# A first batch kept on the chip: block transposes in place of two trips through DRAM in a spectral mixing and feed-forward kernel

## The chip, the cores and the metric

One core of one Trainium2 chip. The metric is the device time in microseconds (us) of one execution. Both kernels were run several times; a run is called fast when it is within 1.5% of the fastest of the same kernel. The engines are TensorE (PE in the profile, PEld for its weight loads), VectorE (DVE), ScalarE (ACT), GpSimd (POOL) and SyncE (SP). A name with a q behind it, such as SPq, is an engine's queue of DMA issues. PSUM is the memory that takes TensorE's products until another engine copies them out, SBUF the one that the engines otherwise read and write. The granted clock is the share of full speed that the profile shows for TensorE.

## The reference, cut to what matters

```python
def _attn_ref(x, filt_r, filt_i):                 # x: 8 batches x 3008 rows x 256 channels
    X = np.fft.rfft(x, axis=1)
    F = (filt_r + 1j * filt_i)[None, :, :]
    y = np.fft.irfft(X * F, n=x.shape[1], axis=1)
    return y.astype(np.float32)

def _moe_ref(x, w_in, w_out, alpha):              # 24064 tokens, 256 -> 2048 -> 256
    h = x @ w_in
    s = np.sin(alpha * h)
    g = h + s * s / (alpha + 1e-09)
    return (g @ w_out).astype(np.float32)
```

The second function is applied to the first one's result. The Fourier transform of length 3008 is split as 47 x 64, so that it becomes matrix products with small tables.

## The kernel before

Each batch goes through four products of the spectral part, and then its rows go through the feed-forward part:

- `first` (profile name `pa<-x`): the transform over 47, for two of the 64 columns at a time;
- `forward` (`pb<-t`): the transform over 64, with the twiddle factors in the table `d_t`. Its 128 output rows are 64 real and 64 imaginary parts;
- the product with the filter on VectorE, then `inverse` (`pc<-p`) with the table `e_t`;
- `last` (`pd<-t`): the inverse transform over 47, which leaves y with the channels on the partitions;
- the feed-forward part: `hidden` (`ph<-y`), a cosine on ScalarE, an add on VectorE, `project` (`po<-v`), in 48 chunks of 16 hidden blocks. A chunk is eight steps of two blocks. One step takes 2.1 to 2.4 us.

Between `first` and `forward`, and between `inverse` and `last`, the axis on the partitions must change. The kernel before does this for every batch with a trip through DRAM: rows are stored in one order (`d<-t`, `d<-g`) and loaded in another (`t<-d`).

```python
        def load_t2(self, g):
            ...
            for p in range(2):
                a0 = p * NS + 6 * g
                eng = nc.gpsimd if self.b else nc.scalar if p else nc.sync
                marks["t2", g] = eng.dma_start(out=self.t2[g][64 * p:64 * p + 64, :, :],
                                               in_=self.d1[a0:a0 + 6, :, :].rearrange("s n c -> n s c"))

        def forward(self, u):
            ...
            nc.scalar.copy(out=self.xf[u], in_=ps)
            if self.fused:
                self.xs[u] = xspool.tile([128, 2, C], FP16, name=f"xs_{b}_{u}", tag="xs")
                for p in range(2):
                    nc.sync.dma_start(out=self.xs[u][64 * p:64 * p + 64, :, :],
                                      in_=self.xf[u][64 - 64 * p:128 - 64 * p, :, :])

        def product(self, u):
            for k in range(1 if self.fused else 2):
                ... tensor_tensor(out=pt, in0=self.xf[u], in1=f_t[k][:, 2 * u:2 * u + 2, :], op=ALU.mult)

        def cross(self, u):                               # only for a fused batch
            xs, p = self.xs[u], self.p[u][0]
            nc.vector.tensor_tensor(out=xs, in0=xs, in1=f_t[1][:, 2 * u:2 * u + 2, :], op=ALU.mult)
            nc.vector.tensor_tensor(out=p, in0=p, in1=xs, op=ALU.add)

        def inverse(self, w):
            ...
            for i in range(2):
                for k, pt in enumerate(pr):               # one product if fused, two if not
                    nc.tensor.matmul(out=ps[:, i, :], lhsT=e_t[:, k, 2 * w + i, :],
                                     rhs=pt[:, i, :], start=(k == 0), stop=(k == len(pr) - 1))
```

A complex product needs each half of the rows (real, imaginary) times the filter's real part, plus the other half times its imaginary part. There are two ways. An **unfused** batch leaves the exchange of the halves to TensorE: the second inverse table has its halves exchanged, which takes 48 inverse products. A **fused** batch exchanges the halves with two DMAs of 64 KB per block (`xs<-xf`), adds on VectorE, and takes 24 inverse products. `FUSED = 2` says that batches 0 and 1 are unfused and the others fused.

Batch 0 stands alone in front of the feed-forward part. The spectral work of batch b then lies between the steps of the feed-forward part for earlier rows, by a table of step numbers:

```python
        for i in range(16):
            put(5 + 0.5 * i if b == 1 else ..., s.first, i, pe=True)
        for g in range(4):
            put(13.5 if b == 1 else max(z + -56, 46.5), s.load_t2, g)
        for u in range(12):
            inv = 22.5 + u if b == 1 else 59 + 2.1 * u if b == 2 else z + -40.8 + 2.3 * u
            fwd = inv - (1.5 if b == 1 else 6)
            put(fwd, s.forward, u, pe=True)
            put(fwd + (0.5 if b == 1 else 1.5), s.product, u)
            if s.fused:
                put(fwd + 4.5, s.cross, u)
            put(inv, s.inverse, u, pe=True)
```

## Time and profile before

| | kernel before |
|---|---|
| time, median of 3 runs | 814.85 us (814.2 to 816.39) |
| span of the profiled run | 812.3 us |
| TensorE busy | 95% of the span |
| first feed-forward product | 53.46 us |
| step 8, first product of the second chunk | 68.10 us |
| last output product | 804.00 us |

The page's first part (busy us, share of the span, instructions) is the first thing to read:

```profile
PE 771.4 (95%) x5649; PEld 527.5 (65%) x5649; DVE 652.4 (80%) x1191; ACT 612.8 (75%) x1200; POOL 65.4 (8%) x111
```

TensorE has only about 41 us in which it is not busy, and most of them lie before step 8. The prediction below shows the other lines. From its marks the kernel divides into four stretches: the start (to the first feed-forward product), the first chunk (to step 8), the long part (to the last output product, 735.9 us), and the tail (8.3 us).

### The profile page before, as it was taken

The page shows a single profiled execution, that of the slowest core. Times are in us where ns is not written, and L with a number is a line of the kernel's source. Part 1 is how long each engine was busy: PE and PEld are TensorE (multiplying, and loading weights), DVE is VectorE, ACT ScalarE, POOL GpSimd, SP SyncE. Part 2 cuts the span into 40 slices and gives each one's busy share as a digit, 9 for nine tenths or more (in the row PEclk, how much of TensorE's full clock was granted, in tenths as well). Part 3 has the DMA queues.
Part 4 walks back from the last instruction along what each step waited for, and adds up shares of the span by engine and source line. Part 5 has one row for each costly group of instructions (what it writes and reads, how often), then busy time and mean ns, then how long its engine had stood idle before and what let it go on. Part 6 is the DMA issues. An engine that isn't in the chain of part 4 may idle for free.

```text
span 812.3 us, 16130 instructions
## 1 busy us (share of the span) xinstructions
PE 771.4 (95%) x5649; PEld 527.5 (65%) x5649; DVE 652.4 (80%) x1191; ACT 612.8 (75%) x1200; POOL 65.4 (8%) x111
## 2 busy tenths in 40 slices
PE   5657999999999999999999999999999999999995
PEld 2324676676666776667667676667667676666674
DVE  3669797789978998789987998779987999777772
ACT  4547787788878888778887887778887887777662
POOL 3210300110020000200002000200002000000000
PEclk9779999999999999999999999999999999999998
DMA  9985755466576465644657554654558333411111
GB/s 213 227 260 132 186 113 148 127 137 141 117 185 149 97 144 126 184 95 95 140 159 178 111 104 116 193 127 104 115 139 214 73 91 84 116 37 40 40 40 46
DMA packets 86201, 104.44 MB, mean 129 GB/s; under 512 B 10388, under 2 KB 72868, under 8 KB 86120
## 3 DMA queue, kind: packets, MB, share of 16 engines
q1 hardware_dynamic: 73904, 73.45, 34.3%
q0 software_dynamic: 10288, 29.11, 18.0%
q10 hardware_dynamic: 1928, 0.86, 0.4%
q8 instruction: 44, 0.72, 0.4%
q14 instruction: 37, 0.30, 0.1%
HBM read 58.02 MB, written 49.81 MB: 133 GB/s over the span
## 4 chain that ended last, share of the span: by engine, by line
PE 88%; DMA 5%; DVE 2%; ACT 2%; issue 1%; POOL 0%; SPq 0%; ACTq 0%; DVEq 0%; POOLq 0%
PE po L383 39%; PE ph L368 38%; PE pa L159 4%; PE pc L210 3%; PE pb L179 3%; PE pd L230 2%; DMA t<-d 2%; DMA x<-in_x_dram 2%; DVE v L372 1%; ACT cos L371 1%; DMA d<-t 1%; ACT t L136 1%; DVE p L193 1%; DMA d<-g 0%; DVE t L138 0%
## 5 line engine op out<-in xcount | busy, mean ns | idle before, releaser
L372 DVE SCALAR_TENSOR_TENSOR v<-cos,ph 128x512 f16<-128x512 f32 (+1 forms) x768 | 483.5, 672 | 119.3 <-ACT cos L371 116.2
L371 ACT ACTIVATE cos<-ph 128x512 f32<-128x512 f32 (+1 forms) x768 | 411.5, 591 | 99.7 <-PE ph L368 98.9
L368 PE MATMUL ph<-y,w 128*128 128x512 f16 (+1 forms) x1536 | 388.5, 375 | 0.8 <-DVE y L138 0.6
L383 PE MATMUL po<-w,v 128*128 128x256 f16 x3008 | 389.0, 272 | 0.0
L383 PEld LDWEIGHTS <-v 128*128 128x128 f16 x3008 | 289.2, 98 | 77.7 <-issue 1.7
L368 PEld LDWEIGHTS <-w 128*128 128x128 f16 x1536 | 148.1, 98 | 104.3 <-issue 3.6
L182 ACT CAST xf<-pb 128x512 f16<-128x512 f32 x96 | 56.9, 594 | 20.4 <-PE pb L179 17.3
L389 ACT COPY o<-po 128x512 f32<-128x512 f32 x96 | 55.6, 579 | 17.9 <-PE po L383 16.3
L136 ACT CAST t<-pa 96x512 f16<-96x512 f32 x88 | 51.2, 585 | 22.8 <-PE pa L159 22.6
L159 PE MATMUL pa<-x,wf_t 94*96 94x512 f16 x128 | 51.0, 408 | 11.7 <-DMA x<-in_x_dram 8.3
L230 PEld LDWEIGHTS <-t 96*128 96x128 f16 x512 | 36.1, 99 | 34.3 <-DMA t<-d 11.0
L170 POOL DMA_DIRECT2D t<-d x56 | 37.0, 676 | 251.1 <-PE ph L368 183.6
L230 PE MATMUL pd<-wi_t,t 96*128 96x94 f16 x512 | 43.0, 208 | 11.5 <-DMA t<-d 10.1
L193 DVE TENSOR_TENSOR p<-xf,filt 128x512 f16<-128x512 f16 x120 | 47.8, 418 | 6.3 <-ACT xf L182 6.1
L136 ACT CAST y<-pd 128x376 f16<-128x376 f32 x82 | 39.3, 480 | 17.0 <-PE pd L230 16.6
L136 ACT CAST g<-pc 128x512 f16<-128x512 f32 x65 | 38.4, 590 | 11.8 <-PE pc L210 11.6
L210 PE MATMUL pc<-p,e_t 128*128 128x256 f16 x240 | 44.0, 278 | 2.7 <-DVE p L193 1.5
L179 PE MATMUL pb<-t,d_t 128*128 128x256 f16 x192 | 38.2, 282 | 5.9 <-DMA t<-d 4.9
L118 POOL DMA_DIRECT2D x<-in_x_dram x32 | 17.0, 536 | 262.8 <-PE pc L210 145.9
L138 DVE CAST t<-pa 96x512 f16<-96x512 f32 x40 | 27.2, 680 | 12.6 <-PE pa L159 12.6
L210 PEld LDWEIGHTS <-e_t 128*128 128x128 f16 x240 | 23.0, 99 | 16.2 <-issue 2.5
L200 DVE TENSOR_TENSOR p<-p,xs 128x512 f16<-128x512 f16 x72 | 30.6, 425 | 2.5
(31 smaller groups left out, 155.2 us busy)
## 6 DMA issues: line engine op xcount, KB each, us to landing
d<-t SPq DMA_DIRECT2D x32, 384.0 KB
d<-g SPq DMA_DIRECT2D x64, 192.0 KB
t<-d SPq DMA_DIRECT2D x32, 384.0 KB
x<-in_x_dram POOLq DMA_DIRECT2D x32, 376.0 KB, 6.2
t<-d POOLq DMA_DIRECT2D x56, 192.0 KB, 7.0
xs<-xf SPq DMA_DIRECT2D x144, 64.0 KB
out_dram<-o SPq DMA_DIRECT2D x72, 94.0 KB
w_in<-in_moe_w_in_dram POOLq DMA_DIRECT2D x2, 1024.0 KB, 8.9
```

The costliest lines, as they stand in the source:

```text
L136: marks["act"] = nc.scalar.copy(out=dst, in_=src)
L159: marks["pe"] = nc.tensor.matmul(out=ps[0:NK, :], lhsT=wf_t, rhs=self.x[ch][:, 2 * j:2 * j + 2, :], start=True, stop=True)
L179: nc.tensor.matmul(out=ps[:, i, :], lhsT=d_t[:, s, :], rhs=self.t2[s // 6][:, s % 6, :], start=True, stop=True)
L182: nc.scalar.copy(out=self.xf[u], in_=ps)
L193: marks["prod", u] = nc.vector.tensor_tensor(out=pt, in0=self.xf[u], in1=f_t[k][:, 2 * u:2 * u + 2, :], op=ALU.mult)
L210: nc.tensor.matmul(out=ps[:, i, :], lhsT=e_t[:, k, 2 * w + i, :], rhs=pt[:, i, :], start=(k == 0), stop=(k == len(pr) - 1))
L230: nc.tensor.matmul(out=psv[:, i, :], lhsT=self.t4[ch][:, 4 * half + i, cb * 128:cb * 128 + 128], rhs=wi_t, start=True, stop=True)
L368: nc.tensor.matmul(out=ps[:, 0:n], lhsT=w1[:, cb, jb * 128:jb * 128 + 128], rhs=y_cols[:, cb, c0:c0 + n], start=(cb == 0), stop=(cb == 1))
L371: nc.scalar.activation(out=cs[:, 0:n], in_=ps[:, 0:n], func=AFT.Sin, bias=float(np.pi / 2))
L372: marks["snake"] = nc.vector.scalar_tensor_tensor(out=v[k][:, jb, 0:n], in0=cs[:, 0:n], scalar=-1.0, in1=ps[:, 0:n], op0=ALU.add, op1=ALU. ...
L383: nc.tensor.matmul(out=pso[k][:, t % 2, :], lhsT=v[k][:, jb, 128 * t:128 * t + 128], rhs=w2[:, jb, :], start=(jb == 0), stop=(jb == 15))
L389: nc.scalar.copy(out=o[:, 0:nb, :], in_=pso[k][:, 0:nb, :])
```

## The change

The intent: take the two DRAM trips of batch 0 out of the start. VectorE transposes 32 x 32 blocks of 4-byte elements (pairs of channels), so batch 0 never leaves the chip. The start is then filled: six PSUM buffers for stage 1, the inverse tables built between its pieces, weights loaded in order of need and scaled on GpSimd and ScalarE, and 14 products without use ("filler") to keep TensorE's clock up. The memory for this is found by dropping the second inverse table after the start, and therefore batch 1 becomes fused. Two more things move: batch 0's last stage takes two products of 64 columns where one of 128 stood, and the short chunk of 384 columns goes from the end of each pair of batches to its middle. The diff, cut to its core (cuts marked by "..."):

```diff
-FUSED = 2
+FUSED = 1
...
-    e_t = cpool.tile([128, 2, NS, 128], FP16)
+    e_t = cpool.tile([128, NS, 128], FP16)
...
     def last(self, u, on_act=None):
             for i in range(4):
-                nc.tensor.matmul(out=psv[:, i, :],
-                                 lhsT=self.t4[ch][:, 4 * half + i, cb * 128:cb * 128 + 128],
-                                 rhs=wi_t, start=True, stop=True)
+                if self.b == 0:
+                    for k in range(2):
+                        nc.tensor.matmul(out=psv[64 * k:64 * k + 64, i, :], lhsT=t4_0[cb][:, n0 + i, :, k],
+                                         rhs=wi0_t, start=True, stop=True)
+                else:
+                    nc.tensor.matmul(out=psv[:, i, :], rhs=wi_t, start=True, stop=True,
+                                     lhsT=t4_h[ch // 2][0:NK, n0 % 16 + i, cb * 128:cb * 128 + 128])
...
-    after(nc.sync.dma_start(out=d_t, in_=d_dram.ap()), marks["x", 1])
+    nc.sync.dma_start(out=d_t, in_=d_dram.ap())
+    x0 = [load_x(0, ch) for ch in range(4)]
...
+    tables = {7: [(0, 0, True), (0, 1, False)], 11: [(0, 2, True), (1, 0, False)], 15: [(1, 1, True), (1, 2, True)]}
+    for i in range(16):
+        own, tag = (fps, "f") if i % 3 == 2 else (hps, "h")
+        ps = own.tile([128, 512], FP32, name=f"pa_0_{i}", tag=tag)
+        nc.tensor.matmul(out=ps, lhsT=wf0_t, rhs=x0[i // 4][:, 2 * (i % 4):2 * (i % 4) + 2, :],
+                         start=True, stop=True)
+        evac(t1_0[:, 2 * i:2 * i + 2], ps.rearrange("p (n c k) -> p n c k", n=2, k=2), i % 2)
+        for e in tables.get(i, ()):
+            inverse_table(*e)
+
+    def turn(dst, src):
+        nc.vector.transpose(out=dst.bitcast(UINT32).rearrange("p s c k -> p c (s k)"),
+                            in_=src.bitcast(UINT32).rearrange("p s c k -> p c (s k)"))
...
-            put(13.5 if b == 1 else max(z + -56, 46.5), s.load_t2, g)
+            put(14.5 if b == 1 else max(z + -56, 46.5), s.load_t2, g)
...
-            inv = 22.5 + u if b == 1 else 59 + 2.1 * u if b == 2 else z + -40.8 + 2.3 * u
-            fwd = inv - (1.5 if b == 1 else 6)
+            inv = 24 + 1.2 * u if b == 1 else 59 + 2.1 * u if b == 2 else z + -40.8 + 2.3 * u
+            fwd = inv - (5 if b == 1 else 6)
```

## The prediction

> **What bounds the kernel now.** I read the page's strip of slices first, then a table by stage, then the timeline of the first 70 us, and last the waits after 80 us.
>
> ```profile
> PE   5657999999999999999999999999999999999995
> PEclk9779999999999999999999999999999999999998
> DMA  9985755466576465644657554654558333411111
> ```
>
> Each digit is a fortieth of the 812.3 us span, 20.3 us. TensorE is busy all the time except in the first three to four slices, where DMA is the full row and the granted clock dips. So the kernel has two parts: a start limited by something else, and a TensorE-bound rest. The table by stage (start:end, length, then busy us and count of PE, PEld, DVE, ACT, POOL, then granted clock, DMA share, GB/s) says so in numbers:
>
> ```profile
> 0.00:12.50 12.50, 4.72 (x10) 1.82 (x11) 1.60 (x4) 4.78 (x8) 6.45 (x16) 1.00 0.86 168
> 12.50:27.50 15.00, 9.45 (x43) 4.44 (x43) 6.64 (x13) 5.83 (x8) 1.11 (x3) 0.81 0.89 237
> 27.50:42.50 15.00, 12.16 (x70) 7.08 (x69) 13.92 (x34) 10.36 (x19) 4.95 (x9) 0.84 1.09 264
> 42.50:53.50 11.00, 2.02 (x20) 1.42 (x19) 5.70 (x10) 1.62 (x4) 1.24 (x2) 0.65 0.80 219
> 53.50:68.10 14.60, 11.38 (x61) 5.13 (x61) 12.69 (x27) 11.57 (x23) 2.02 (x4) 0.91 0.98 248
> 80.00:804.00 724.00, 720.90 (x5382) 500.80 (x5379) 601.48 (x1084) 569.75 (x1122) 49.62 (x80) 1.00 0.50 120
> ```
>
> From 80 to 804 us TensorE lacks 3.1 us in all. Nothing that leaves its instruction stream alone can win more than that there. The reserve lies before 68 us. The chain that ended last (start us, us, what) shows what ends each pause, and the timeline of TensorE where the next part starts:
>
> ```profile
> 17.52 4.90 DMA d<-t
> 22.58 4.31 DMA t<-d
> 44.08 3.19 DMA d<-g
> 47.49 3.84 DMA t<-d
> 53.43 10.46 DMA x<-in_x_dram
> ```
> ```profile
> 53.46 1.87 PE L368 MATMUL ph<-y,w 128*128 128x512 f16 x4 [0.17 <-ACT y L136]
> ...
> 68.10 1.03 PE L368 MATMUL ph<-y,w 128*128 128x512 f16 x4
> ```
>
> The first four lines are batch 0's two trips through DRAM: 9.5 us between stage 1 and the forward transform, 7.8 us between inverse and last stage. The feed-forward part starts at 53.46 us, and its second chunk (step 8, the first with output products between) at 68.1 us.
>
> **What the Trainium skill says.**
> (1) "VectorE: DVE Perf Modes", section "The three transpose paths": VectorE transposes only inside 32x32 blocks, 311 ns for 128x128 bf16 against 390 ns on TensorE. "Vector Engine (DVE) Microarchitecture Reference", section 3.8, adds one element per cycle and lane. No transpose of this kind is in the trace of before. Estimate for 1024 elements at 0.96 GHz: 1.07 us, plus the fixed part of that 311 ns figure (311 - 133 = 178 ns), about 1.2 us.
> (2) "GPSIMD Engine Reference", section 3.1: an fp32 tensor_tensor of 2048 elements takes 4497 ns, about twice VectorE. Estimate: 2.2 ns each, 1.7 us for 768 elements. The trace has no GpSimd arithmetic, so no run shows it yet; VectorE's own product in this role took 681 ns for 512.
> (3) "TensorE: Matmul & The Clock Gate", Part 1: after an idle window of about 3.4 us the array runs at half clock. The trace agrees: granted clock 0.65 from 42.5 to 53.5 us, and four products took 1.87 us at 53.46 but 1.03 us at 68.10.
>
> **The change part by part.**
>
> *Stage 1.* All products of batch 0 use six PSUM buffers, copies alternate between ScalarE and VectorE, and the results stay in SBUF. In before, loads that wait for a free slot show the four x pieces landed by 6.5, 8.3, 10.1 and 12.2 us. The middle table is now loaded beside them from the start; the engines land 0.21 MB of fp16 per us of such casting loads (209 to 212 GB/s), so read 0.42 MB, and the last piece lands near 12.5. Then four products, two copies each on ScalarE (0.58) and VectorE (0.69): the last copy ends near 15.0. The inverse tables (six groups; four on ScalarE at 1.02 us as before) lie between pieces and end near 18 on TensorE and ScalarE, beside the block transposes.
>
> *First DRAM trip removed, block transposes added.* VectorE: 2 x 1.2, a filter copy of 3072 elements (0.55 us for 1536 before; slope 0.4, so 0.95), 2 x 1.2, another 0.95: 6.7 us, 15.0 to 21.7. Before had 17.5 to 27.0. The filters (3.15 MB of fp32 source behind x) need until about 20; the first half is in time.
>
> *Forward, products, inverse.* Per block of four columns: 2 VectorE products at 0.355 us (spacing in runs: 2.09 us for 6), 1 + 3/4 ScalarE copies at 0.54 us (1.07 for 2), 12 TensorE products of 128 columns at about 0.08 (8 table transposes took 0.62). VectorE from 21.7: 24 x 0.355 + 2 x 0.69 = 9.9; ScalarE 21 x 0.54 = 11.3 from about 19; TensorE 144 x 0.08 = 11.5. All three are near each other, so I add 2 us for hand-overs: the last product ends at 33.6. Before, the same stage ran from 27.0 to 42.8, with 8 filter copies (4.4 us) on a VectorE that was 93% busy.
>
> *Second trip removed.* VectorE: 2 x 1.2, the last inverse copy 0.69, 2 x 1.2, then 0.5 us for the last transform and 0.55 for its copy: 6.6 us. The feed-forward part starts at 40.2 instead of 53.46: 13.3 us won. The filler products fill the gaps there and keep the clock; they are followed by waits anyway, so they cost nothing.
>
> *Weights.* The alpha broadcast and w_in start when the filters have landed (about 20.5 us); 1.05 + 2.1 MB, beside 0.8 MB of filter copies, at 350 GB/s come by about 32, w_out by 39. GpSimd scales w_in after the last product: 5 x 1.7 + 0.6 = 9.1 us, 33.8 to 42.9. One catch: the alpha rows sit in the buffer that the cosines overwrite, so the fourth cosine waits for the last scaling. At 40.2 + 2.4 = 42.6 that just fits.
>
> *First chunk.* Before, 14.6 us from its first product to step 8, with VectorE carrying 14 activations at 0.64 us, evictions and 12 scalings of w_out (3.4 us). These scalings go to GpSimd and ScalarE. After: ScalarE 14 cosines x 0.54, six evictions of about 0.5, four scalings near 0.35, 1.3 us to start: about 12.5 us. 2.1 us won. x of batch 1 is asked for when GpSimd is through, about 43, and its first piece lands 5 us later (4.9 before): 48, just before TensorE wants it at step 6 (49). Before, TensorE stood 2.1 us for it.
>
> *The long part.* Batch 1 becomes fused: 24 products of 256 columns fewer, 24 x 0.109 = 2.6 us of TensorE won; VectorE has 12 x 0.42 = 5 us more, with 20% idle. Batch 0's last stage doubles its matmuls (48 more at perhaps 0.04, a fifth of it after step 8): 0.4 us lost. Schedule shifts: 0.5 of the 3.1 us idle. The short chunk moves from the end to the middle of each pair, so the final copy is 512 wide instead of 256 and more rows are stored after it: 1 us lost.
>
> Sum: 13.3 + 2.1 + 2.6 - 0.4 + 0.5 - 1.0 = 17.1 us. 814.85 - 17.1 = 797.7; I say 797.5.
>
> **The rivals.**
> A. GpSimd is slower than the page's figure. At 3 us for 768 elements it would end near 50, the fourth cosine would wait 7 us and x of batch 1 would come 7 us late, in the same stretch: about 803 to 805. For it: no row of the trace supports the 1.7 us, and the output is fp16. Against: transposes and activations have one SBUF input each; "SBUF - State Buffer", section "Who interferes with whom", says those do not contend with GpSimd.
> B. The strided copies. Stage 1 and inverse copies now write 4-byte pairs 128 bytes apart; if they took half as long again, 28 copies over two engines would add about 4 us: 801.
> C. A cold TensorE in the forward stage: the pause between stage 1 and the first forward product is short, but at half clock 144 products cost about 0.12 instead of 0.08: 5 us, 802. Against: in before the clock came back 3 to 5 us after the stage began.
> D. Batch 1's DRAM trip stalls TensorE: loads come at step 14.5, and the first forward product at 19 instead of 21. That leaves about 9 us for a trip that took 9.5: up to 3 us lost, 800.
> E. The start is better tuned than my sum of serial steps, with fewer hand-over losses (2 us) and more of the idle time after 68 us removed (up to 3 us): 792 to 793.
>
> **Range and chances.** A to D lose 3 to 7 us each and are each less likely than not; E wins 5. One or two may combine: 789 to 806 should hold it 8 times in 10. The border of 2% is at 798.6, one microsecond above my number, so the chances are nearly even: 0.53 faster, 0.46 the same, 0.01 slower. The first part cannot grow past its old length, since both trips are gone.
>
> **What would show it.** Right: first feed-forward product at 39 to 42 us, step 8 at 51 to 55, four block transposes in a row near 1.2 us each, clock 1.0 in the first chunk, TensorE idle for at most 3 us between step 8 and the end, 24 inverse products in batch 1. Wrong: GpSimd products well over 1.7 us, cosines released by GpSimd, TensorE waiting for x of batch 1 or for the t loads, copies into strided pairs above 0.7 us. If the first feed-forward product stands after 46 us, the sum of the start is what failed.

## The result

| | before | after |
|---|---|---|
| time, median of 4 runs of the same rounds | 815.25 us (814.2 to 816.39) | 810.76 us (809.3 to 811.39) |
| span of the profiled run | 812.3 us | 809.6 us |

The ratio is 0.9942, with a 95% interval of 0.9922 to 0.9962. All ratios here are the mean time of one kernel's fast runs over the mean of the other's in the same rounds, so not quite the ratio of the medians. The change is faster by 0.6%: within the 2% that the prediction held nearly as likely as more, but 13 us off its number and outside its range.

The strip of slices of the kernel after, to be set against the first fence of the prediction:

```profile
PE   4799898999999999999999999999999999999995
PEclk9799999999999999999999999999999999999998
DMA  9943657555476454845465555654656243411111
```

The start is denser, as intended: the third slice has 9 where before had 5. But the fifth and the seventh slice (81 to 101 and 121 to 142 us), nines before, now hold an 8, and this is the place to look. I cut both traces at the same marks: step 8, the first product of the third chunk (index 2), that of the sixth (index 5), and the last output product. The table by stage has the columns start:end, length, then busy us and count of PE, PEld, DVE, ACT and POOL, granted clock, DMA share, GB/s. Before:

```profile
68.10:86.75 18.65, 17.56 (x128) 11.47 (x126) 15.71 (x31) 13.90 (x28) 0.00 (x0) 1.00 0.43 121
86.75:139.17 52.42, 52.09 (x385) 36.60 (x383) 43.15 (x81) 41.86 (x82) 7.39 (x12) 1.00 0.63 148
139.17:804.00 664.83, 662.06 (x4947) 459.52 (x4944) 553.03 (x996) 522.56 (x1029) 42.23 (x68) 1.00 0.49 118
```

After, with the first chunk in front:

```profile
44.02:57.98 13.96, 12.80 (x93) 6.78 (x91) 11.18 (x19) 11.70 (x26) 12.53 (x15) 1.00 0.60 112
57.98:76.57 18.59, 18.06 (x121) 11.50 (x119) 14.33 (x24) 16.02 (x33) 0.00 (x0) 1.00 0.28 82
76.57:135.00 58.43, 53.09 (x377) 35.17 (x374) 47.22 (x94) 41.55 (x82) 7.39 (x12) 1.00 0.60 136
135.00:800.53 665.53, 662.65 (x4955) 460.47 (x4953) 554.60 (x998) 523.25 (x1032) 41.70 (x68) 1.00 0.49 120
```

The middle stretch, three chunks of the same width in both kernels, went from 52.4 to 58.4 us. TensorE's work in it grew by 1.0 us, its idle time from 0.33 (52.42 - 52.09) to 5.34 us (58.43 - 53.09). The ledger of the two profiled runs:

| stretch | before | after | measured | predicted |
|---|---|---|---|---|
| start | 53.46 | 44.02 | -9.4 | -13.3 |
| first chunk | 14.64 | 13.96 | -0.7 | -2.1 |
| long part | 735.90 | 742.55 | +6.6 | -2.7 |
| tail | 8.31 | 9.08 | +0.8 | +1.0 |
| sum | 812.3 | 809.6 | -2.7 | -17.1 |

(The medians differ by 4.5 us and these two profiled runs by 2.7; the runs of either of these two kernels lie up to 2.2 us apart.) The long part is what gave the gain back. Its 6.6 us are 4.6 us more idle time of TensorE (4.19 to 8.75 us, by the sums of the busy times above) and 2.1 us more work (731.7 to 733.8).

**The idle time.** The timeline of the kernel after (start us, us, engine, line, operation, tiles, count, and in brackets the idle time just before and what ended it). First, batch 1's loads behind its DRAM trip, and the first product that needs them:

```profile
79.17 5.26 POOL L182 DMA_DIRECT2D t<-d  x8 [22.59 <-DMA out_dram<-o]
...
86.89 0.38 PE L190 MATMUL pb<-t,d_t 128*128 128x256 f16 x2 [2.63 <-DMA t<-d]
```

The loads were issued from 79.17 us on; TensorE reached the product at 84.26, and the data came 2.63 us later. Then a chain of four lines some 30 us later:

```profile
112.35 4.34 SPq L197 DMA_DIRECT2D xs<-xf  x6
...
116.91 0.42 DVE L210 TENSOR_TENSOR xs<-xs,filt 128x512 f16<-128x512 f16 x1 [2.24 <-DMA xs<-xf]
116.91 0.59 ACT L193 CAST xf<-pb 128x512 f16<-128x512 f32 x1 [3.15 <-DMA xs<-xf]
...
117.55 0.38 PE L190 MATMUL pb<-t,d_t 128*128 128x256 f16 x2 [1.05 <-ACT xf L193]
```

Read from the bottom: TensorE waits for a PSUM buffer that ScalarE has not copied out; ScalarE stands 3.15 us because the buffer it wants to write is still being read by an exchange; and SyncE's queue takes 4.34 us to issue six of those. This is a third DMA trip that batch 1 did not have before. Four more pauses close the list: 0.5 us each at 117.93 and 125.82 us (behind VectorE, in the same chain), 1.57 us at 139.52 us, where `last` of batch 1 waits for its data from DRAM, and 1.06 us at 161.64 us, where `forward` of batch 2 waits for its loads.

**The work.** The groups of instructions by shape (line, engine, operation, shapes, count, then busy us and mean ns of one, then idle time before) of the kernel after:

```profile
L248 PE MATMUL pd<-wi_t,t_h 96*128 96x94 f16 x448 | 37.2, 204 | 1.6 <-DMA t_h<-d 1.6
L245 PE MATMUL pd<-wi_t,t_h 128*64 128x94 f16 x128 | 10.7, 303 | 0.4 <-DVE t_h L330 0.4
L330 DVE STREAM_TRANSPOSE t_h<-t_h 128x1024 uint32<-128x1024 uint32 x4 | 4.7, 1221 | 0.1
```

128 products of 64 columns were busy for 10.7 us, 0.084 each. That is as long as a whole product takes (37.2 us for 448, 0.083), and two of them stand for one. They cost double. But 64 columns alone don't make a product slow: the same trace has other pairs of 64 columns, the transposes of the inverse table, and these are fast:

```profile
17.07 1.08 PE L310 MATMUL pse<-id,d_t 128*64 128x128 f16 x32
...
64.14 0.70 PE L245 MATMUL pd<-wi_t,t_h 128*64 128x94 f16 x8
```

At L310 the two of a pair start 4 ns apart, and one pair follows the other after 56 ns, as whole products of 128 columns do there (L307, 55 ns). At L245 the two also start together, but after step 8 the next pair comes after about 130 ns, and a weight load takes 214 ns instead of 110. By the code, the 64 columns of L310 are adjacent in memory, while those of L245 (`t4_0[cb][:, n0 + i, :, k]`) lie 128 bytes apart. That the distance makes the difference is likely and was not tested alone: the right-hand operands differ too (128 and 94 columns).

**The start.** The timeline of the kernel after:

```profile
16.10 1.04 PE L322 MATMUL pa<-x,wf_t 94*128 94x512 f16 x4
...
18.27 2.37 DVE L330 STREAM_TRANSPOSE t_h<-t 128x1024 uint32<-128x1024 uint32 x2
...
25.05 1.10 DVE L361 TENSOR_TENSOR p<-xf,filt 128x512 f16<-128x512 f16 x3
...
57.98 1.04 PE L460 MATMUL ph<-y,w 128*128 128x512 f16 x4
```

The first block transpose starts at 18.27 us where the prediction has 15.0. The last four products of stage 1 began at 16.10, behind the tables' transposes; the last piece of x had landed at 14.96.

### The profile page after: what moved, and what is told of

Its sections match the earlier page's. It is cut to its first block, busy times and chain, and to the rows that moved or that the text cites. A ratio compares the mean times of both kernels' runs of the same rounds, so it can differ in the third digit from the quotient of the medians.

```text
span 809.6 us, 16470 instructions
## 1 busy us (share of the span) xinstructions
PE 775.8 (96%) x5815; PEld 535.7 (66%) x5815; DVE 658.4 (81%) x1185; ACT 615.5 (76%) x1206; POOL 76.4 (9%) x116
## 3 DMA queue, kind: packets, MB, share of 16 engines
q0 software_dynamic: 9120, 25.70, 16.7%
## 4 chain that ended last, share of the span: by engine, by line
PE 86%; DMA 4%; DVE 2%; ACT 2%; issue 1%; SPq 0%; POOL 0%; ACTq 0%; DVEq 0%
PE po L475 38%; PE ph L460 37%; PE pa L170 3%; PE pd L248 2%; PE pb L190 2%; PE pc L221 2%; DMA t<-d 2%; DMA xs<-xf 1%; DVE v L464 1%; PE pd L245 1%; ACT cos_all L463 1%; DMA t_h<-d 1%; SPq L493 0%; ACT w L442 0%; DVE t_h L330 0%
## 5 line engine op out<-in xcount | busy, mean ns | idle before, releaser
L464 DVE SCALAR_TENSOR_TENSOR v<-cos_all,ph 128x512 f16<-128x512 f32 (+1 forms) x768 | 482.9, 671 | 113.2 <-ACT cos_all L463 107.8
L463 ACT ACTIVATE cos_all<-ph 128x512 f32<-128x512 f32 (+1 forms) x768 | 411.0, 592 | 98.5 <-PE ph L460 96.9
L149 ACT CAST t_h<-pa 96x512 f16<-96x512 f32 x73 | 42.8, 586 | 9.1 <-PE pa L170 8.9
L248 PEld LDWEIGHTS <-t_h 96*128 96x128 f16 x448 | 31.3, 97 | 19.8 <-DMA t_h<-d 2.0
L170 PE MATMUL pa<-x,wf_t 94*96 94x512 f16 x112 | 42.7, 381 | 1.5 <-ACT y L149 1.2
L248 PE MATMUL pd<-wi_t,t_h 96*128 96x94 f16 x448 | 37.2, 204 | 1.6 <-DMA t_h<-d 1.6
L210 DVE TENSOR_TENSOR xs<-xs,filt 128x512 f16<-128x512 f16 x84 | 35.1, 418 | 3.9 <-DMA xs<-xf 3.8
L204 DVE TENSOR_TENSOR p<-xf,filt 128x512 f16<-128x512 f16 x84 | 35.1, 418 | 2.1 <-ACT xf L193 2.1
L221 PE MATMUL pc<-p,e_t 128*128 128x256 f16 x168 | 32.1, 273 | 1.0 <-DVE p L211 0.6
L151 DVE CAST t_h<-pa 96x512 f16<-96x512 f32 x39 | 26.5, 680 | 0.6 <-PE pa L170 0.5
```

The lines of the kernel that those rows point to most:

```text
L149: marks["act"] = nc.scalar.copy(out=dst, in_=src)
L170: marks["pe"] = nc.tensor.matmul(out=ps[0:NK, :], lhsT=wf_t, rhs=self.x[ch][:, 2 * j:2 * j + 2, :], start=True, stop=True)
L221: nc.tensor.matmul(out=ps[:, i, :], lhsT=e_t[:, 2 * w + i, :], rhs=pt[:, i, :], start=(k == 0), stop=(k == len(pr) - 1))
L248: nc.tensor.matmul(out=psv[:, i, :], rhs=wi_t, start=True, stop=True, lhsT=t4_h[ch // 2][0:NK, n0 % 16 + i, cb * 128:cb * 128 + 128])
L463: nc.scalar.activation(out=cs[:, 0:n], in_=ps[:, 0:n], func=AFT.Sin, bias=float(np.pi / 2))
L464: marks["snake"] = nc.vector.scalar_tensor_tensor(out=v[k][:, jb, 0:n], in0=cs[:, 0:n], scalar=-1.0, in1=ps[:, 0:n], op0=ALU.add, op1=ALU. ...
```

## The experiments

All 12 kernels gave correct results and ran in five rounds each against the kernel before. Times are medians; "idle" is that of TensorE between step 8 and the last output product (after: 8.75 us). One caution for single profiles: six kernels with practically the same start (after, e1, e2, e7, e9, e10) had their first feed-forward product at 42.6 to 44.5 us, so a difference under 2 us in the start is not read from one profile.

The theory: the idle time in the long part comes from batch 1, namely (a) its loads stand too few steps ahead of its forward products, and (b) its fusion put a third DMA trip on a SyncE queue that is nearly full. The rivals: the short chunk's new place costs time; the fillers do; or the work on GpSimd delays batch 1. The last has no run of its own; the trace of the kernel after speaks against it, since GpSimd ended its scalings at 56.6 us and then stood idle for 22.6 us before it issued batch 1's loads.

### e1: batch 1's forward products two steps later (undoes a)

```diff
-            fwd = inv - (5 if b == 1 else 6)
+            fwd = inv - (3 if b == 1 else 6)
...
-                put(fwd + (3 if b == 1 else 4.5), s.cross, u)
+                put(fwd + (2.5 if b == 1 else 4.5), s.cross, u)
```

> The changed kernel, only batch 1's forward products start two steps later (step 21 instead of 19, same spacing, inverse unchanged, cross product half a step closer). Theory 1 (the early gain is given back because batch 1's DRAM trip is too short in steps, so TensorE stands 2.63 us for the t load): that wait falls to under 0.6 us, the feed-forward chunk 3 starts 2 us earlier than in the changed kernel's trace, total about 808.5. Rival (the TensorE pauses there come from a shortage of VectorE and ScalarE, the named load is only the last to come): the pause moves to the products or the next chunk, idle of TensorE from 58 us to the end stays at 8 to 9 us, total within 0.7 us of 810.8.

Measured: 814.46 us (813.3 to 814.68), ratio 0.9988 [0.9976, 1.0]. This missed. The wait for the loads is gone, but idle rose to 12.4 us, and the timeline shows where:

```profile
99.80 0.39 PE L221 MATMUL pc<-p,e_t 128*128 128x256 f16 x2 [1.28 <-DVE p L211]
103.48 0.39 PE L221 MATMUL pc<-p,e_t 128*128 128x256 f16 x2 [1.34 <-DVE p L211]
```

There are ten such waits of 0.4 to 1.3 us: the inverse product waits for the sum on VectorE, which waits for the exchange. Three steps between `forward` and `inverse` are too few for the exchange. So with the inverse fixed in place, the schedule has no room for both trips: the five steps that the change gave to the exchange were taken from the loads. (a) and (b) are one budget.

### e4: the kernel before with batch 1 fused (b alone)

```diff
-FUSED = 2
+FUSED = 1
...
-            fwd = inv - (1.5 if b == 1 else 6)
+            fwd = inv - (4.5 if b == 1 else 6)
...
-                put(fwd + 4.5, s.cross, u)
+                put(fwd + (3 if b == 1 else 4.5), s.cross, u)
```

> The kernel before, only batch 1 fused (half the inverse matmuls, exchange of halves by DMA, forward products from step 18 so that they stand 4.5 steps after the t loads, as in the changed kernel). Prediction's term (24 products of 256 columns fewer are 2.6 us won): 812 to 813, TensorE idle after 68 us stays near 4.2 us. Theory 2 (at this place in the schedule the fused form costs its gain again in waits for the t load and for the exchange): TensorE's inverse products after 68 us shrink by 2.5 us, but its idle time grows by 2 to 5 us: 815 to 818.

Measured: 828.8 us (828.62 to 830.77), ratio 1.0175 [1.0162, 1.0188]: 14 us slower than before. TensorE's inverse work after step 8 did fall by 2.3 us, and its idle time rose from 4.2 to 16.7. The timeline:

```profile
104.25 10.78 SPq L186 DMA_DIRECT2D xs<-xf  x8
...
112.97 0.58 ACT L182 CAST xf<-pb 128x512 f16<-128x512 f32 x1 [6.22 <-DMA xs<-xf]
113.60 0.59 PE L179 MATMUL pb<-t,d_t 128*128 128x256 f16 x2 [5.40 <-ACT xf L182]
```

It is the same chain as in the kernel after, larger: eight exchanges took 10.8 us in the queue and TensorE stood 5.4 us in one piece. Fusing batch 1 costs time by itself, without any block transposes. The size is not that of the changed kernel: here batch 1's trip was also shortened (`forward` from step 18, a wait of 2.7 us), so this shows the mechanism and not the amount. Nor is all of the 14 us waiting: TensorE's work after step 8 also grew, by 2.3 us, and the granted clock was 0.50 from 106.3 to 116.5 us, in the midst of the waits.

### e10: the exchange issued from GpSimd's queue (SyncE's queue alone)

```diff
-                    nc.sync.dma_start(out=self.xs[u][64 * p:64 * p + 64, :, :],
+                    (nc.gpsimd if b == 1 else nc.sync).dma_start(out=self.xs[u][64 * p:64 * p + 64, :, :],
```

> The changed kernel, batch 1 still fused, but its exchange of halves is issued by GpSimd's queue instead of SyncE's. In the changed kernel's trace SyncE is 91% taken from 88 to 123 us, with 23 exchange issues of 0.57 us. Theory 2a (SyncE's issue time is what makes the exchange late): waits for the exchange (ScalarE 3.2, VectorE 3.8 us) vanish, TensorE's idle in chunk 4 falls from 2.4 to under 1 us, the 2.6 us wait for t stays: total 809 to 809.8. Rival 2b (the DMA engines or the trip's own length): the waits stay or grow, total 810.5 or more.

Measured: 808.29 us (806.72 to 809.41), ratio 0.9913 [0.9899, 0.9927]. The middle stretch against the kernel after's 58.43 us, and the first forward product:

```profile
77.06:132.07 55.01, 51.99 (x376) 35.37 (x374) 47.36 (x94) 41.56 (x82) 19.86 (x36) 1.00 0.64 144
```
```profile
86.88 0.38 PE L190 MATMUL pb<-t,d_t 128*128 128x256 f16 x2 [2.12 <-DMA t<-d]
```

The same bytes move, fewer us pass: 55.0 instead of 58.4. ScalarE and VectorE waited 0.7 us for the exchange instead of 6.8, the wait for the loads stays at 2.1. So what hurt in (b) was not the transfer, but its turn in SyncE's queue. (By the times alone the gain is less sure: the intervals of the two ratios, 0.9899 to 0.9927 and 0.9922 to 0.9962, just touch.) Worked out from the issue records of the kernel after, that queue was issuing DMAs for 0.72 of the time from 88 to 123 us (23 exchanges of 0.57 us, 19 stores of 0.47 and 4 of 0.63), against 0.44 from 96 to 120 us before. The 91% of the expectation also counts 7.3 us of semaphore instructions, and the longest of these, 2.3 us for one, look like waits.

### e7: batch 1 unfused again, forward products from step 22.5 (undoes a and b)

The second inverse table is kept in the half of y that batch 1 fills later.

```diff
-FUSED = 1
+FUSED = 2
...
+    e1_part = [y[:, cb, 1].rearrange("p n r -> p (n r)")[:, 0:n * 128].rearrange("p (s c) -> p s c", c=128)
+               for cb, n in ((0, 16), (1, 8))]
...
-        put(13 + i, negate, i)
+        put(39 + i, negate, i)
...
-            inv = 24 + 1.2 * u if b == 1 else ...
-            fwd = inv - (5 if b == 1 else 6)
+            inv = 24 + 1.1 * u if b == 1 else ...
+            fwd = inv - (1.5 if b == 1 else 6)
```

> The changed kernel with batch 1 unfused again (24 more inverse matmuls, no exchange of halves by DMA; second inverse table kept in the part of y that batch 1 fills later; forward from step 22.5, 8 steps after the t loads). Theory 2 (the early gain was given back by the third DMA trip that fusing put into batch 1): the start is unchanged at 44, TensorE's idle time after step 8 falls from 8.75 to under 3 us, its inverse work grows by 2.6 us: total about 807 to 808. Prediction's view (fusing is 2.6 us of TensorE won): 812.5 to 813.5. Rival (the pauses come from the earlier start alone, x and t of batch 1 late whatever its form): idle stays above 6 us, total 812 or more.

Measured: 805.77 us (804.74 to 807.77), ratio 0.9885 [0.9869, 0.99]; the kernel after's interval, 0.9922 to 0.9962, does not touch it. The middle stretch:

```profile
76.01:130.82 54.81, 54.49 (x400) 37.52 (x398) 43.10 (x81) 41.52 (x82) 7.38 (x12) 1.00 0.54 120
```

Idle fell there from 5.34 to 0.32 us, and in the whole long part from 8.75 to 2.57. The inverse products cost 2.9 us more (18.5 to 21.5), near the 24 x 0.11 expected. So fusing batch 1 saved close to 3 us of work and cost about 6 us of waiting, the loads' wait included.

### e9: unfused, but forward products from step 19 (undoes b, keeps a)

As e7, with

```diff
-            inv = 24 + 1.1 * u if b == 1 else ...
+            inv = 20.5 + 1.2 * u if b == 1 else ...
```

> As e7 (batch 1 unfused) but with its forward products from step 19, where the changed kernel has them, and the inverse 1.5 steps behind. Splits what e7 mended. If the t load is late for the step whatever the form: TensorE waits again 2 to 3 us for t at the first forward product, the waits for the exchange stay away, idle after step 8 about 5 us, total 807.5 to 808.5. If the t load is late only because of the fused form's traffic: no such wait, total as e7 (805.8).

Measured: 809.36 us (807.43 to 809.99), ratio 0.9922 [0.9909, 0.9935]. The exchange's waits are gone, the wait for the loads is back in the same place, and the time is 3.6 us above e7's:

```profile
86.47 0.38 PE L190 MATMUL pb<-t,d_t 128*128 128x256 f16 x2 [2.18 <-DMA t<-d]
```

So each cause leaves its own wait: e9 and e10 have no exchange in SyncE's queue and keep the wait for the loads; e1 gives the loads their steps and keeps waits for the exchange; only e7 has neither. The wait itself is not the whole of the 3.6 us. In the profiles, e9's long part is 3.1 us longer than e7's, 1.5 by idle time and 1.6 by work, and its granted clock was 0.50 from 87.8 to 91.2 us, just behind the wait; e7's was 1.00 all through the long part.

### e2: the short chunk back at the end for the later pairs (rival)

```diff
-    chunks = [(pb, c0, 384 if c0 == 2560 else 512) for pb in range(B // 2)
-              for c0 in [*range(0, 2561, 512), *range(2944, 2 * S, 512)]]
+    chunks = [(pb, c0, min(512, 2 * S - c0) if pb else 384 if c0 == 2560 else 512) for pb in range(B // 2)
+              for c0 in (range(0, 2 * S, 512) if pb else [*range(0, 2561, 512), *range(2944, 2 * S, 512)])]
```

(and odd batches from 3 on two steps earlier, as before).

> The changed kernel, only the 384 wide chunk put back at the end of pairs 1 to 3 (pair 0 as changed), with the odd batches two steps earlier there as before. The prediction's term says the move costs 1.0 us at the end (in the traces 9.1 instead of 8.3 us from the last output product to the end): 809.8 to 810.3, last chunk 17.6 us instead of 21.0 but the chunks before longer by as much. Rival: no difference beyond 0.3 us, or slower by 1 us because the odd batches' deadlines come earlier again.

Measured: 812.98 us (810.35 to 818.06), ratio 0.9979 [0.9954, 1.0005]. The tail was 0.3 us shorter (8.81 against 9.08), but pauses came at 232.75 us (1.42), 326.34 (0.60) and 424.44 (0.86), of which the kernel before has the first two at nearly the same places (239.03 and 329.93), and the long part was 2.4 us longer. So the move of the short chunk is no cause of the loss. By the medians and the profiles it is a gain of some 2 us, for which the prediction had a loss of 1; the intervals of e2 and of the kernel after overlap.

### e3: without the 14 filler products (rival)

```diff
-    warm_pe(6)
     s0.last(0, True)
     s0.last(2, False)
-    warm_pe(8)
```

> The changed kernel without the 14 filler products. Theory 4: the granted clock falls to half in the gap before the feed-forward part, its first products take 0.4 us instead of 0.2 until about 3 us in, but ScalarE and VectorE set the pace of the first chunk, so step 8 moves by 0 to 1 us and the total by less than 1 us: 810.8 to 811.8. Rival: the fillers themselves delay the last transforms (they stand ahead of them in TensorE's order), so without them the start comes 0.5 us earlier and the total is the same or better.

Measured: 811.76 us (809.97 to 814.34), ratio 0.9956 [0.994, 0.9972]. The first chunk took 15.44 us instead of 13.96, and the granted clock was 0.50 from 40.5 to 47.3 us, where the kernel after had 1.00. No cost of the fillers shows, and in the profile they save about 1.5 us in the first chunk; in the times, with overlapping intervals, a gain of 1 us is not resolved.

### e5 and e6: the end of stage 1

e5 builds all inverse tables after the third forward block, on ScalarE, instead of between the pieces of stage 1. e6 is e5 with the middle table's load waiting for a piece of x, as the kernel before had it:

```diff
-        for e in tables.get(i, ()):
-            inverse_table(*e)
...
             forward_0(i)
+            if i == 2:
+                for g in range(3):
+                    for k in range(2):
+                        inverse_table(k, g, True)
...
-    nc.sync.dma_start(out=d_t, in_=d_dram.ap())                            # e6 only
     x0 = [load_x(0, ch) for ch in range(4)]
+    after(nc.sync.dma_start(out=d_t, in_=d_dram.ap()), marks["x", 1])      # e6 only
```

> The changed kernel, the inverse tables all built after the third forward block on ScalarE, none between stage 1 pieces. The start in the changed kernel came 3.8 us later than predicted, nearly all of it by the end of stage 1 (first block transpose at 18.27 instead of 15.0). Theory 3a (the table transposes stand in TensorE's order before the last four pieces): first block transpose at about 16.8, feed-forward part up to 1.5 us earlier if ScalarE is not made late by six tables in a row (6.1 us), otherwise about equal. Theory 3b (x lands late because the table load shares the DMA engines): first block transpose moves by under 0.7 us.

> As e5, and the middle table's load waits for the second piece of x, as in the kernel before. Theory 3b: the pieces of x land 2 us earlier (first product of stage 1 at about 6.3 instead of 8.4), the first block transpose at 14.5 to 15.5. The filters and the tables then come as late as before or later, so the feed-forward part starts only 1 to 2 us earlier: 42 to 43; total 809 to 810. Rival: DMA bytes up to the filters are the same and the filter copy waits for them, start unchanged at 44.

Measured: e5 809.0 us (807.7 to 811.28), ratio 0.9925 [0.9912, 0.9938]; e6 809.17 us (806.35 to 809.87), ratio 0.9921 [0.9907, 0.9935]. The first feed-forward product stood at 43.35 us in e5, within the spread of the unchanged start, and at 41.07 in e6. The timeline of e6 has the transposes four us earlier than the kernel after:

```profile
14.30 2.37 DVE L328 STREAM_TRANSPOSE t_h<-t 128x1024 uint32<-128x1024 uint32 x2 [0.38 <-ACT t L149]
```

x's last piece had landed at 11.96 instead of 14.96 us. In both e5 and e6 the first transpose follows 2.3 us behind the last piece of x (14.39 and 16.71 us in e5), in the kernel after 3.3. So the order of the loads was the larger part of the late start (2.4 us, the tables about 1), and with it mended the start comes within 0.9 us of the predicted 40.2. But e6's median is no lower than e5's: its profiled run was its fastest, 2.8 us under the median. Where the other runs lost it, no trace shows. Their mean granted clocks were lower (0.994 to 0.996, where the fastest has 0.997), and the next run suggests that it was again in batch 1's waits.

### e8: e6 and e7 together

> Both mends: e6 (x ahead of the middle table, inverse tables late) and e7 (batch 1 unfused). If the start and the pauses of batch 1 are separate terms, their gains add: e6 gained 1.6 us by the medians (start 3 us earlier), e7 3 us by theory 2: total 804 to 806. If an earlier start only lengthens the wait in batch 1, no better than e7.

Measured: 803.69 us (803.48 to 803.91), ratio 0.9856 [0.9843, 0.9869]. Start at 40.99 us, idle 2.33. Here the earlier start is in the time: 2.1 us under e7, with a start 2.4 us earlier. The runs also lie closer together than any other kernel's, within 0.5 us.

### e11: batch 0's last stage with whole products again

The transposes back write rows of 128 channels in natural order, so that one product of 128 columns can take them. The edit changes two things at once: one product stands for two, and its columns lie side by side in memory.

```diff
-                    for k in range(2):
-                        nc.tensor.matmul(out=psv[64 * k:64 * k + 64, i, :], lhsT=t4_0[cb][:, n0 + i, :, k],
-                                         rhs=wi0_t, start=True, stop=True)
+                    nc.tensor.matmul(out=psv[:, i, :], lhsT=t4_0[cb][:, n0 + i].rearrange("p c k -> p (c k)"),
+                                     rhs=wi0_t, start=True, stop=True)
...
-        nc.vector.transpose(out=dst.bitcast(UINT32).rearrange("p s c k -> p c (s k)"),
-                            in_=src.bitcast(UINT32).rearrange("p s c k -> p c (s k)"))
+        nc.vector.transpose(out=dst.bitcast(UINT32)[:, :, :, 0].rearrange("p s c -> p c s"),
+                            in_=src.bitcast(UINT32)[:, :, :, 0].rearrange("p s c -> p c s"))
```

> The changed kernel, the block transposes write the back-turned data in rows of 128 channels (each 4-byte pair 256 bytes from the one before in the transpose's order), so that batch 0's last stage takes one matmul of 128 columns instead of two of 64. Theory 5 (the two halves cost 78 ns each against 42 ns for one whole): 16 groups of 8 become 16 of 4; after step 8 five groups save 0.45 us each and 0.1 us on the product before each: 2.7 us, total 808 to 808.5, if the strided block transposes keep their 1.18 us. If the strided write slows them to 2.3 us, the start is 4.5 us later and the total 812 to 813.

Measured: 812.64 us (808.05 to 815.24), ratio 0.9969 [0.9945, 0.9992]: no better than the kernel after. By shape:

```profile
L333 DVE STREAM_TRANSPOSE t_h<-t_h 128x1024 uint32<-128x1024 uint32 x4 | 7.5, 1938 | 0.1
...
L244 PE MATMUL pd<-wi_t,t_h 128*128 128x94 f16 x64 | 5.6, 215 | 2.1 <-DVE t_h L333 1.8 <-DVE t_h L151 0.2
```

The products halved, 5.6 us for 10.7. The four transposes, which now write with a stride, took 1.94 us each instead of 1.22, and two of them lie on the path to the feed-forward part: it began at 45.60. The first chunk made up for that (12.24 us instead of 13.96; part of this may be GpSimd's head start with the weights), step 8 came at 57.84 against 57.98, and then the wait for batch 1's loads was 3.1 us instead of 2.6. In this profiled run TensorE's idle time after step 8 grew by 1.9 us, and its work by 1.9 us as well, although the last transforms took 2.0 us less. The granted clock fits the growth of the work: it fell to half within the wait for the loads, and once more (143.6 to 147.0 us) behind the wait of `last`.

```profile
85.60:92.42 6.82, 5.92 (x27) 3.64 (x28) 1.80 (x3) 2.73 (x5) 0.00 (x0) 0.50 0.70 161
```

So with the waits in place, the saved work was lost again to waiting and to the clock. The runs fit this: the fastest, 808.05 us, is the only one with a mean clock of 0.990 and has the time that was expected; the other five have 0.983 to 0.986.

### e12: e8 and e11 together

> e8 (x first, tables late, batch 1 unfused) with e11's rows. If terms add: 803.7 minus 2.7 = 801; with slow strided transposes 804 to 806.

Measured: 802.45 us (802.06 to 802.97), ratio 0.9845 [0.9832, 0.9857], the best of all and 8.3 us under the kernel after. The first chunk and the middle stretch:

```profile
43.45:55.69 12.24, 10.30 (x67) 4.56 (x65) 10.52 (x18) 11.27 (x25) 10.39 (x14) 1.00 0.70 127
...
74.71:127.35 52.64, 52.32 (x385) 36.32 (x382) 43.07 (x81) 41.45 (x82) 7.39 (x12) 1.00 0.57 125
```

From step 8 to the last output product e12 took 735.2 us and e8 737.7: without the waits, the whole products are worth 2.5 us there, of which the slower transposes take back 0.7 by step 8 (55.69 against 54.97). Its interval overlaps e8's, so that e12 beats e8 rests on the medians (1.2 us) and on this profile. The middle stretch is now as short as before's 52.42.

## Why the prediction was wrong, point by point

**What bounds the kernel: right.** The start could be cut, and TensorE's stream sets the rest. The view that held this, 3.1 us of idle time from 80 to 804 us, was read as "nothing can be won there". It should also have been read as "much can be lost there": a change of schedule in that part had almost only the losing side.

**Start, 13.3 us: 9.4 came.** The mis-sized term is the end of stage 1, "the last copy ends near 15.0": the first block transpose came at 18.27. The step "the last piece lands near 12.5" failed with 14.96 (the middle table's 0.79 MB moved ahead of x; e6 gets 11.96 with the old order). The steps behind it held well: transposes 1.22 us each (predicted 1.2), from the first transpose to the first product 6.8 us (6.7), products to their end at 37.54 us 12.5 (11.9 with the 2 us for hand-overs), from there to the feed-forward part 6.5 (6.6).

**First chunk, 2.1 us: 0.7 came.** "About 12.5 us" became 13.96. The four w_out scalings on ScalarE took 0.42 us each, not far from the predicted 0.35. TensorE had become the fuller engine: 12.80 us busy of 13.96, against ScalarE's 11.70. Seven groups of 64-column products stand there, and with whole ones (e11, e12) TensorE was busy for 10.30 and the chunk took 12.24.

**The long part, 2.7 us won: 6.6 lost.** This is the step that failed. Its terms:

- "24 x 0.109 = 2.6 us of TensorE won": right as work. The inverse products after step 8 went from 21.0 to 18.5 us. As time it was wrong, since e7, which gives the work back, is 5 us faster.
- "Schedule shifts: 0.5 of the 3.1 us idle", as a gain: the idle time grew by 4.6 us. Rival D had named one of its causes, with the right place and a fair size (up to 3 us; 2.63 measured), but it stood among the rivals as less likely than not, and its amount was not in the sum. The other, that fusing batch 1 adds an exchange to SyncE's queue and binds five steps of the schedule, appears nowhere in the prediction: fusion was booked as VectorE and TensorE work only.
- "0.4 us lost" for the 64-column products: about 2.7. The prediction took "perhaps 0.04" for each product more, and "a fifth" of the 48 after step 8; by the table of steps it is five of twelve groups, 20 products. From the start of one to the start of the next, the 40 of them after step 8 took 78 ns each, 3.12 us; 20 whole ones at the 42.5 ns that they took before would be 0.85. That is 2.3 us. Another 0.5 us lies in the hidden product ahead of each of the five groups: 309 ns to the next product instead of 216. In front of each group the weight loads pause for 0.42 us, which they don't in front of whole products. e12, which has whole products, shows 0.99 us and 216 ns in their place. What was mis-sized is the pair: with adjacent columns two halves took no longer than one whole (L310), with columns 128 bytes apart more than twice as long.

The remaining growth of the work is not explained: the hidden products took 2.2 us more in all, 213.4 ns on the mean of 1504 instead of 211.9, of which only the 0.5 above is placed. In e7, without most of the waits, they took 0.8 us less than in the kernel after.

**Tail, 1.0 us lost: 0.8.** The number is near, but the cause named holds for only a part: e2, which has the narrow final copy again, is 0.3 us shorter there than the kernel after. The other 0.5 is not explained, so the agreement is in part luck. And the short chunk's move as a whole was no loss (e2).

**The rivals.** A, slow GpSimd: no. Its six scalings took 9.63 us (9.1 predicted), and the fourth cosine waited 0.5 us for it. B, strided copies: no, 0.61 to 0.69 us each, where before had 0.59 on ScalarE and 0.69 on VectorE. C, a cold TensorE: in part. The granted clock was 0.57 from 20 to 30 us, and the products took 0.107 us each until about 31.5, then 0.055; the 12.5 us for the stage hold this. D: yes, and it was half of the story. E: no.

**The range.** It gave rival D up to 3 us and let "one or two" rivals combine. Four misses came together, all on one side: the late start (3.9 us), the first chunk (1.4), the idle time (0.5 won became 4.6 lost, 5.1) and the work (2.2 won became 2.1 lost, 4.3, of which 2.3 by the 64-column products). They make 14.7; less 0.2 for the tail, that is the difference between the predicted 17.1 and the 2.7 of the profiled runs. What stays open: whether the distance of the columns alone makes the 64-column products slow, and why their weight loads did not lie behind the product ahead of them; why the hidden products took 1.5 ns more each; and where e6's other runs lost its early start.

## What to carry to other kernels

When a tuned schedule has no idle time left, count a moved or added DMA trip in steps of the schedule (issue, transfer, consumer) before counting the work it saves; here some 3 us of saved products cost 6 us of waits, and the same bytes issued from another queue cost about 2.5 us less. A wait can cost more than its length: in the profiles of e3, e4, e9 and e11 the granted clock fell to half around the waits, for 3.4 us in e3 and e9 and 10.2 us in all in e4 and e11, while in those of the kernel after and of e10 waits of 2.6 and 2.1 us left it at 1.00. A gain at the start only reaches the end if the next producer keeps its lead: measure both at common marks along the kernel, not by the total. Two products with half the columns can cost as much as one whole or more than twice as much (56 and about 130 ns a pair here): look at the time of one group of each form, with the same layout in memory, in a trace before splitting.

## What the Trainium skill lacked or had wrong

- "VectorE: DVE Perf Modes", "The three transpose paths": its figure is for 128x128 bf16. It has none for 4-byte elements with a strided output. Here 1024 elements per partition took 1.22 us with contiguous writes and 1.94 us with rows written at a stride (e11). The estimate for the contiguous form made from the page (1.2 us) was right.
- "TensorE: Matmul & The Clock Gate", "Weight-path perf modes": it says that the fast weight load is on only when the number of weights is 128. This fits that: in the kernel after, loads of 128 columns took a mean of 97 to 98 ns in the long part, of 96 columns 123 ns, and of 64 adjacent columns 110 ns, so fewer columns did not load faster. What the page lacks is a figure for columns that lie apart: loads of 64 columns 128 bytes apart took 214 ns, their pairs followed each other after about 130 ns instead of 56, and the product ahead of a group took 309 ns instead of 216.
- "GPSIMD Engine Reference", section 3.1: the estimate from its fp32 figure, 9.1 us for the six scalings, agreed with 9.63. It has no figure for instructions as short as 256 elements (its 769 ns for 512 is a best case): the one-input form with a scalar per partition took 0.9 us for 256 fp32 elements (eight in 7.23 us), 3.5 ns per element where the page's 2048 elements with two inputs come to 2.2.
- "DMA: Bandwidth & Descriptors", "Issuing engines are not separate DMA queues": it says that issuing from several engines saves only the sequencer's time to initiate the DMA, "which is usually small relative to the DMA itself". What it saves is what e10 shows; but here it was not small: an exchange of 64 KB took 0.57 us of SyncE's queue (0.52 of GpSimd's), the queue was issuing for 0.72 of the time, and moving 24 exchanges to another engine won 2.5 us by the medians. The page has no figure for the queue time of one such DMA as a whole.
